# A hand-ordered RWKV-6 + SwiGLU kernel on one Trainium2 core: another order of the steps of its list

## The chip, the cores and the metric

The kernel runs on 1 core of one Trainium2 (trn2) chip. The metric is the device time of one execution in microseconds (us). Where the text names an engine by a short name, PE is TensorE (matmuls; PEld its weight loads), DVE is VectorE, ACT is ScalarE, POOL is GpSimd and SP is SyncE, which here only issues transfers.

## The reference

For every batch b (4), head h (8) and time t (768), with vectors r, k, v, w of 48 elements, an attention with a decaying state:

```python
for t in range(S):
    cur = np.einsum('bhd,bhe->bhde', u[None] * kt, vt)
    y[:, :, t] = np.einsum('bhd,bhde->bhe', rt, state + cur)
    state = wt[:, :, :, None] * state + np.einsum('bhd,bhe->bhde', kt, vt)
```

Then y, laid out as 3072 tokens of 384 features, goes through an RMS norm with gain and a SwiGLU network with 1536 hidden units:

```python
xn = x / np.sqrt(np.mean(x * x, -1, keepdims=True) + 1e-06) * rms_g
g = xn @ w_gate
out = (g * (1 / (1 + np.exp(-g))) * (xn @ w_val)) @ w_out
```

## The kernel before

Time is cut into 6 superblocks n = 0 to 5 of 128 steps; a superblock holds the 4 batches j = 0 to 3, so 512 tokens. In a superblock the attention goes batch by batch: the running sum of ln w becomes a matmul with a triangular mask (`ln`, `cs_mm`), its exponentials scale r and k (`exp_r`, `exp_k`, `r_mul`, `k_mul`), both are transposed (`rk_pe` and `rk_tr`), q k^T is formed and masked (`q_mm`, `q_mask_e`, `q_mask_o`), and `y_mm` adds the part of the block itself and the part of the carried state (`st_mm`, `st_new` make the next state). The u-term goes by POOL (`bonus_mul`, `bonus_v`) with a sum on DVE (`bonus_sum`). `x_add`, `x_sq`, `x_rstd`, `xn_mul`, `xn_pe`, `xn_out` make the normed and transposed tokens. When all four batches of a superblock have these, its network starts: 12 pairs of `gate_mm` and `val_mm` (three matmuls of 512 columns each), `silu` on ACT, `h_mul` on DVE, then `o_mm` (12 matmuls) for each batch, `o_out` and `out_dma`. The attention of superblock n+1 is woven into the network of superblock n.

Everything goes in the order of one list: `ORDER` (L25 to L126) has one word for each step, function.n.j, and L648 calls them one after the other. No scheduler moves anything. Each engine keeps the order of the steps that are its own, and waits, at its next step, for whatever that step's inputs and buffers need; nothing behind it on that engine passes. So the list sets five queues at once:

- SP issues the loads of r, k, v (L211) and w (L228), 192 KB each, the transposes by DMA of superblocks 2 to 5, and the stores.
- POOL issues the weights of the network (`load_gv`, L313: gate and value; `load_wo`, L319: w_out in three parts), between its own work: `bonus_mul` (L423, L424), `bonus_v` (L433), `q_mask_o` (L476), from superblock 2 on the casts of v. The `load_wo` also wait until load_v.1.1 has landed.
- PE's PSUM buffers come from three pools: `psA` (2, for gate and cs), `psB` (2, for val and cs) and `psQ` (4, for all the rest). A pool hands its buffers out in turn, in the order of the list: a step that takes a psQ buffer waits until the taker four before it has been read out.
- In superblocks 0 and 1 the casts of v (`cast_v`, L337) and the copies of the transposes out of PSUM (`rk_tr`, L449) are ACT's, and the norm's `x_rstd` of superblock 0 also (two small activations on L198). All exp, ln and silu are recorded on L198, their table loads on L196.
- DVE does `w_tot` (L409), `r_mul` (L412), `k_mul` (L417), `bonus_sum` (L428), `q_mask_e` (L465), `q_mask_o` of superblock 0 (L473), `st_new` (L492 and L494), `x_add` (L511), `xn_out` (L551), `h_mul` (L584) and half of `o_out` (L636).

The calls of `load_wo`, and the wait that goes with them:

```python
WO_BEHIND = (('load_v', 1, 1), ('load_v', 1, 1), ('load_v', 1, 1))
```

## Time and profile before

| | us |
|---|---|
| median of 6 runs | 207.83 |
| lowest and highest run | 206.96, 208.36 |
| the profiled execution: its own time | 208.21 |
| the profiled execution: its span, first to last instruction | 206.5 |

So 1.71 us of the profiled execution lie around its span, and that execution is 0.38 us above the median. Its mean granted TensorE clock is 0.958 of full speed.

The steps can be placed on the trace, since each engine keeps the order of the list. The marks that matter here, in us from the start of the span: the first network starts (gate_mm.0.0) at 28.60; the second part of its weights is used first (gate_mm.0.4) at 37.12; the last gate (gate_mm.0.11) at 49.97 to 50.78; its first `o_mm` starts at 53.77; the second network starts at 65.25, the third at 95.06, the fourth at 124.97, the fifth at 153.11, the sixth at 171.94; the last matmul ends at 203.3.

How to read it: the profile gives each engine's busy time, in 40 slices of the span too; the view by stages gives the same for stretches that the reader chooses; the chain of waits goes back from the last instruction to what released each one; the DMA view gives what each queue moved in a stretch (q1 carries what SP issues, q0 what POOL issues).

### The profile page before, as it was taken

The numbers are of one execution on the slowest core, as the hardware profiler recorded it, in microseconds if no ns is written. First come the engines' busy times: TensorE is split into PE (matmuls) and PEld (weight loads), VectorE is DVE, ScalarE is ACT, GpSimd is POOL, SyncE is SP. The second block draws the span as 40 slices with busy tenths as digits, with TensorE's granted clock in tenths as the row PEclk, the third lists the DMA queues.
The fourth block names the chain that finished last, engine by engine and source line by source line (L and its number), as shares of the span: only waits on it lengthen the run. The fifth ranks groups of instructions, "written<-read, shape, count | busy, mean of one in ns | idle before, by whom it ended". The sixth has DMA issues, their size and how long they took to land.

```text
span 206.5 us, 4369 instructions
## 1 busy us (share of the span) xinstructions
PE 191.2 (93%) x1524; PEld 111.2 (54%) x1524; DVE 158.6 (77%) x323; ACT 138.4 (67%) x282; POOL 108.1 (52%) x167
## 2 busy tenths in 40 slices
PE   4667889898999999999999999999999999999993
...
DVE  6498845778999899999999989899997955246411
...
PEclk9995558999999999999999999999999999999999
...
GB/s 133 218 212 202 185 201 203 175 166 227 186 204 223 177 211 229 207 235 201 170 212 251 122 185 211 202 233 106 38 153 203 42 38 3 76 0 40 0 119 76
DMA packets 125728, 32.41 MB, mean 157 GB/s; under 512 B 120581, under 2 KB 124553, under 8 KB 125705
## 3 DMA queue, kind: packets, MB, share of 16 engines
...
## 4 chain that ended last, share of the span: by engine, by line
PE 71%; SPq 19%; ACT 3%; DMA 3%; issue 1%; DVE 1%; ACTq 0%; DVEq 0%
PE ps_q L629 21%; PE ps_a L566 20%; PE ps_b L566 19%; SPq L211 16%; SPq L228 3%; DMA rt<-in_r_dram 3%; PE ps_q L458 2%; PE ps_q L503 2%; PE ps_q L506 2%; PE ps_a L378 1%; PE ps_q L486 1%; PE ps_q L540 1%; ACT lw L198 1%; ACT L196 1%; PE ps_a L381 1%
## 5 line engine op out<-in xcount | busy, mean ns | idle before, releaser
L584 DVE TENSOR_TENSOR ht<-ps_b,sg 128x512 bf16<-128x512 f32 x72 | 49.0, 688 | 20.6 <-PE ps_b L566 14.3
L198 ACT ACTIVATE sg<-ps_a 128x512 bf16<-128x512 f32 x72 | 42.9, 597 | 32.9 <-PE ps_a L566 30.3
L566 PE MATMUL ps_a<-xnt,wg_sb 128*128 128x512 bf16 x216 | 59.7, 386 | 1.0 <-DMA wg_sb<-in_moe_w_gate_dram 1.0
L566 PE MATMUL ps_b<-xnt,wv_sb 128*128 128x512 bf16 x216 | 59.2, 383 | 0.0
L629 PE MATMUL ps_q<-wo_sb,ht 128*128 128x384 bf16 (+1 forms) x300 | 50.1, 319 | 0.0
L629 PEld LDWEIGHTS <-ht 128*128 128x128 bf16 x300 | 28.0, 97 | 16.4
L423 POOL TENSOR_TENSOR ruk<-rt,kt 128x384 f32<-128x384 f32 x24 | 24.6, 1024 | 22.9 <-DMA rt<-in_r_dram 14.2
L566 PEld LDWEIGHTS <-wv_sb 128*128 128x128 bf16 x216 | 23.7, 114 | 20.9 <-issue 2.0
L566 PEld LDWEIGHTS <-wg_sb 128*128 128x128 bf16 x216 | 23.3, 115 | 21.3 <-issue 1.8
L424 POOL TENSOR_TENSOR ruk<-ruk,u_bc 128x384 f32<-128x384 f32 x24 | 23.9, 998 | 1.9
L476 POOL TENSOR_SCALAR_AFFINE_SELECT qts<-qts 128x512 bf16<-128x512 bf16 x20 | 12.7, 634 | 15.6 <-ACT qts L469 15.6
L433 POOL TENSOR_TENSOR ydiag<-vt,diag 128x384 f32<-128x384 f32 x24 | 19.8, 829 | 0.6 <-DVE diag L428 0.5
L465 DVE TENSOR_TENSOR qts<-ps_q,mask_lt 128x512 bf16<-128x512 f32 x24 | 16.4, 683 | 2.1 <-PE ps_q L460 1.7
L529 ACT ACTIVATE xn<-xb,rstd 128x384 bf16<-128x384 f32 x24 | 14.4, 608 | 2.1 <-POOL rstd L525 1.9
L198 ACT ACTIVATE lw<-wt 128x384 bf16<-128x384 f32 x24 | 12.1, 517 | 4.6 <-DMA wt<-in_w_dram 4.6
L469 ACT CAST qts<-ps_q 128x512 bf16<-128x512 f32 x20 | 11.6, 582 | 4.5 <-PE ps_q L460 4.5
L511 DVE TENSOR_TENSOR xb<-ps_q,ydiag 128x384 f32<-128x384 f32 x24 | 13.2, 551 | 1.8 <-PE ps_q L506 1.7
L196 ACT ACT_TABLE_LOAD x10 | 12.8, 1283 | 1.8 <-PEq L665 1.6
L636 DVE COPY ob<-ps_q 128x384 f32<-128x384 f32 (+1 forms) x13 | 7.0, 539 | 8.5 <-PE ps_q L629 8.5
L516 ACT ACTIVATE junk<-xb 128x384 bf16<-128x384 f32 x24 | 12.5, 519 | 1.5 <-DVE xb L511 1.2
L428 DVE TENSOR_REDUCE diag<-ruk 128x8 f32<-128x384 f32 x24 | 12.9, 544 | 0.0
L417 DVE TENSOR_TENSOR rk<-kt,ps_b 128x384 bf16<-128x384 f32 x20 | 11.0, 548 | 2.4 <-ACT ps_b L198 2.1
...
## 6 DMA issues: line engine op xcount, KB each, us to landing
...
```

What stands on the lines that cost most here:

```text
L196: nc.scalar.preload_act_table_set(table_name)
L198: return nc.scalar.activation(**kw).ins
L211: dmas["load_" + which, n, j] = nc.sync.dma_start(out=inp[which, n, j], in_=t[j, :, n * L:(n + 1) * L, :].rearrange("h t d -> t h d")).ins
L423: nc.gpsimd.tensor_tensor(out=ruk[n, j], in0=inp["r", n, j], in1=inp["k", n, j], op=ALU.mult)
L424: nc.gpsimd.tensor_tensor(out=ruk[n, j], in0=ruk[n, j], in1=u_bc, op=ALU.mult)
L433: nc.gpsimd.tensor_tensor(out=ydiag[n, j], in0=inp["v", n, j], in1=diag[n, j].to_broadcast([128, H, D]), op=ALU.mult)
L465: nc.vector.tensor_tensor(out=qts[n, j][:, 0], in0=bank["q", n, j][0], in1=bc_mid(mask_lt, NP), op=ALU.mult)
L511: nc.vector.tensor_tensor(out=xb[n, j], in0=bank.pop(("y", n, j)), in1=ydiag[n, j].rearrange("p h d -> p (h d)"), op=ALU.add)
L529: nc.scalar.activation(out=xn, in_=xb[n, j], func=AF.Copy, scale=rstd[n, j][:, 1:2])
L566: nc.tensor.matmul(ps, lhsT=units(ws, c, f), rhs=xnt[n][:, c, :], start=(c == 0), stop=(c == KC - 1))
L584: nc.vector.tensor_tensor(out=ht[n][:, f, :], in0=bank.pop(("v", n, f)), in1=bank.pop(("sg", n, f)), op=ALU.mult)
L629: nc.tensor.matmul(ps[:, cols], lhsT=ht[n][:, f, b * L:(b + 1) * L], rhs=wo_sb[:, f, cols], start=(f == 0), stop=(f == FC - 1))
```

## The change

The list `ORDER` is written anew; it has the same 1063 steps, and nothing else in the kernel changes. Line numbers behind the list move down by one. By engine:

- SP: the first 26 loads (through load_v.1.1) keep their order. Then load_r.1.2, load_k.1.2, load_r.1.3, load_k.1.3 come in this order, where before both k came first. load_v.1.2 goes ahead of load_w.2.1; load_k.2.0 and load_w.2.2 go ahead of load_v.1.3; load_r.2.0 goes from ahead of load_w.2.1 to behind load_v.1.3; the transpose rk_tr.2.0 goes from ahead of load_k.2.2 to behind load_k.2.3. Later, out_dma.3.2 and 3.3 go behind the four xn_tr of superblock 5.
- POOL: the order is the same through bonus_mul.1.0, all four `load_gv` included. Then bonus_v.1.0 comes ahead of bonus_mul.1.1; load_wo.0.0 comes right behind bonus_mul.1.1, and load_wo.2.0 and load_wo.1.0 come behind bonus_mul.1.2 (before: 2.0 and 1.0 ahead of bonus_mul.1.2, and 0.0 behind q_mask_o.1.0); bonus_mul.1.3 comes ahead of q_mask_o.1.0 and q_mask_o.1.1.
- ACT: exp_r.1.0 goes forward by 12 places, to behind cast_v.0.1; x_sq.0.0 goes behind both; ln.1.1 goes behind x_rstd.0.0; cast_v.0.2 goes behind rk_tr.0.3 and cast_v.0.3 behind exp_k.1.0 and x_sq.0.1; ln.1.3 goes ahead of x_rstd.0.2; exp_r.1.2 ahead of exp_k.1.2. In the first network rk_tr.1.0 comes ahead of silu.0.3. Later ln.2.3 goes behind xn_mul.1.3. The number of table loads stays 10.
- DVE: in superblock 0 q_mask_e.0.1, w_tot.0.2, q_mask_o.0.1 and bonus_sum.0.1 come ahead of x_add.0.0; st_new.0.1 and x_add.0.1 ahead of bonus_sum.0.2. In the first network the steps of superblock 1 follow the new order of the loads: before, k_mul.1.2, k_mul.1.3, r_mul.1.2, st_new.1.0, r_mul.1.3 follow each other, with h_mul steps between; now r_mul.1.2, k_mul.1.2, r_mul.1.3, st_new.1.0, k_mul.1.3.
- PE: st_mm.0.1 and y_mm.0.1 come ahead of rk_pe.0.3 and q_mm.0.2; st_mm.0.3 goes from ahead of cs_mm.1.2 to behind gate_mm.0.1; q_mm.1.0 goes ahead of gate_mm.0.4; rk_pe.1.1 goes behind val_mm.0.7, rk_pe.1.3 and st_mm.1.1 behind gate_mm.0.10; cs_mm.2.1 goes behind y_mm.1.3; q_mm.2.0 goes behind val_mm.1.1. In superblocks 2 to 4 y_mm.2.0, y_mm.3.0 and q_mm.3.2 come 7 to 11 places earlier and a few others move by 1 to 5; from gate_mm.4.0 on, o_mm.4.1 and o_mm.4.2 move by 1 and 3 places and the rest by one at most.
- At the end o_out.4.1 goes from behind silu.5.1 to behind silu.5.10, and o_out.4.2 from behind h_mul.5.6 to behind h_mul.5.11.

The part of the diff for superblocks 0 and 1:

```diff
@@ ORDER, superblocks 0 and 1 @@
-load_w.0.0 load_v.0.0 load_w.0.1 load_k.0.0 load_r.0.0 ln.0.0 load_w.0.2 load_r.0.1 ln.0.1 cs_mm.0.0 load_k.0.1
-cs_mm.0.1 exp_k.0.0 load_w.0.3 exp_r.0.0 k_mul.0.0 bonus_mul.0.0 exp_r.0.1 r_mul.0.0 exp_k.0.1 load_r.0.2 w_tot.0.0
-cast_v.0.0 rk_pe.0.0 ln.0.2 load_k.0.2 st_mm.0.0 r_mul.0.1 rk_tr.0.0 cs_mm.0.2 load_w.1.0 st_new.0.0 bonus_mul.0.1
-q_mm.0.0 k_mul.0.1 load_v.0.1 w_tot.0.1 bonus_sum.0.0 ln.0.3 rk_pe.0.1 exp_k.0.2 q_mask_e.0.0 load_k.0.3 exp_r.0.2
-cs_mm.0.3 q_mask_o.0.0 bonus_v.0.0 rk_tr.0.1 load_r.0.3 y_mm.0.0 k_mul.0.2 bonus_mul.0.2 exp_k.0.3 q_mm.0.1 load_w.1.1
-r_mul.0.2 exp_r.0.3 x_add.0.0 ln.1.0 rk_pe.0.2 load_v.0.2 bonus_sum.0.1 x_sq.0.0 q_mask_e.0.1 cast_v.0.1 bonus_v.0.1
-load_v.0.3 w_tot.0.2 rk_tr.0.2 q_mask_o.0.1 cs_mm.1.0 k_mul.0.3 load_w.1.2 q_mm.0.2 bonus_sum.0.2 bonus_mul.0.3
-r_mul.0.3 load_k.1.0 q_mask_o.0.2 ln.1.1 rk_pe.0.3 x_rstd.0.0 load_w.1.3 cast_v.0.2 y_mm.0.1 bonus_v.0.2 rk_tr.0.3
-load_r.1.0 x_add.0.1 load_gv.0.0 q_mask_e.0.2 cast_v.0.3 load_r.1.1 xn_mul.0.0 bonus_sum.0.3 load_gv.0.1 q_mm.0.3
-ln.1.2 y_mm.0.2 bonus_v.0.3 x_sq.0.1 q_mask_e.0.3 st_mm.0.1 exp_k.1.0 w_tot.0.3 x_add.0.2 load_gv.1.1 cs_mm.1.1
-x_rstd.0.1 q_mask_o.0.3 exp_r.1.0 load_gv.1.0 x_sq.0.2 y_mm.0.3 exp_k.1.1 xn_pe.0.0 x_add.0.3 st_mm.0.2 x_rstd.0.2
-st_new.0.1 xn_mul.0.1 x_sq.0.3 st_new.0.2 st_mm.0.3 load_v.1.0 cs_mm.1.2 x_rstd.0.3 xn_out.0.0 xn_mul.0.2 xn_pe.0.1
-xn_mul.0.3 xn_out.0.1 xn_pe.0.2 ln.1.3 xn_pe.0.3 xn_out.0.2 exp_r.1.1 xn_out.0.3 exp_k.1.2 cs_mm.1.3 k_mul.1.0
-exp_r.1.2 gate_mm.0.0 st_new.0.3 exp_k.1.3 exp_r.1.3 val_mm.0.0 silu.0.0 gate_mm.0.1 h_mul.0.0 val_mm.0.1 silu.0.1
-gate_mm.0.2 h_mul.0.1 val_mm.0.2 silu.0.2 gate_mm.0.3 val_mm.0.3 load_k.1.1 silu.0.3 load_v.1.1 r_mul.1.0
-bonus_mul.1.0 load_k.1.2 h_mul.0.2 rk_pe.1.0 gate_mm.0.4 h_mul.0.3 load_k.1.3 rk_tr.1.0 r_mul.1.1 val_mm.0.4
-load_r.1.2 silu.0.4 bonus_sum.1.0 gate_mm.0.5 bonus_mul.1.1 k_mul.1.1 q_mm.1.0 load_r.1.3 silu.0.5 val_mm.0.5
-h_mul.0.4 cast_v.1.0 load_w.2.0 q_mask_e.1.0 gate_mm.0.6 q_copy_o.1.0 load_wo.2.0 h_mul.0.5 rk_pe.1.1 load_r.2.0
-st_mm.1.0 k_mul.1.2 val_mm.0.6 load_wo.1.0 rk_tr.1.1 k_mul.1.3 gate_mm.0.7 bonus_mul.1.2 silu.0.6 r_mul.1.2 val_mm.0.7
-silu.0.7 h_mul.0.6 gate_mm.0.8 cast_v.1.1 load_w.2.1 st_new.1.0 rk_pe.1.2 bonus_v.1.0 val_mm.0.8 rk_tr.1.2 q_mm.1.1
-h_mul.0.7 q_mask_o.1.0 gate_mm.0.9 silu.0.8 r_mul.1.3 load_wo.0.0 q_copy_o.1.1 val_mm.0.9 bonus_sum.1.1 silu.0.9
-rk_pe.1.3 h_mul.0.8 bonus_v.1.1 st_mm.1.1 gate_mm.0.10 rk_tr.1.3 q_mask_e.1.1 bonus_mul.1.3 load_v.1.2 val_mm.0.10
-h_mul.0.9 silu.0.10 st_new.1.1 gate_mm.0.11 y_mm.1.0 silu.0.11 q_mm.1.2 q_mask_o.1.1 x_add.1.0 ln.2.0 val_mm.0.11
-q_mask_e.1.2 load_v.1.3 q_mm.1.3 h_mul.0.10 y_mm.1.1 load_k.2.0 h_mul.0.11 q_copy_o.1.2 cs_mm.2.0 bonus_sum.1.2
-x_sq.1.0 q_mask_o.1.2 o_mm.0.0 load_k.2.1 bonus_sum.1.3 q_copy_o.1.3 x_rstd.1.0 x_add.1.1 ln.2.1 load_w.2.2
-q_mask_e.1.3 exp_r.2.0 q_mask_o.1.3 cast_v.1.2 r_mul.2.0 load_w.2.3 cs_mm.2.1 x_sq.1.1 bonus_v.1.2 o_out.0.0 st_mm.1.2
-xn_mul.1.0 y_mm.1.2 st_new.1.2 x_rstd.1.1 load_r.2.1 o_mm.0.1 cast_v.1.3 bonus_mul.2.0 xn_mul.1.1 load_r.2.2 x_add.1.2
-exp_k.2.0 x_sq.1.2 k_mul.2.0 st_mm.1.3 y_mm.1.3 exp_r.2.1 st_new.1.3 rk_tr.2.0 o_mm.0.2 o_out.0.1 bonus_v.1.3
-exp_k.2.1 ln.2.2 x_rstd.1.2 x_add.1.3 ln.2.3 load_k.2.2 w_tot.2.0 k_mul.2.1 load_r.2.3 xn_pe.1.0 xn_mul.1.2 xn_pe.1.1
-o_out.0.2 cs_mm.2.2 x_sq.1.3 xn_out.1.0 xn_pe.1.2 load_k.2.3 o_mm.0.3 exp_r.2.2 w_tot.2.1 x_rstd.1.3 xn_out.1.1
-exp_k.2.2 load_v.2.0 r_mul.2.1 bonus_mul.2.1 xn_mul.1.3 r_mul.2.2 out_dma.0.0 xn_out.1.2 xn_pe.1.3 cs_mm.2.3 w_tot.2.2
-xn_out.1.3 q_mm.2.0 rk_tr.2.1 exp_k.2.3 k_mul.2.2 gate_mm.1.0 bonus_mul.2.2 exp_r.2.3 bonus_sum.2.0 val_mm.1.0
...
+load_w.0.0 load_v.0.0 load_w.0.1 load_k.0.0 load_r.0.0 ln.0.0 load_w.0.2 load_r.0.1 cs_mm.0.0 ln.0.1 load_k.0.1
+cs_mm.0.1 exp_k.0.0 exp_r.0.0 load_w.0.3 k_mul.0.0 exp_r.0.1 bonus_mul.0.0 r_mul.0.0 exp_k.0.1 w_tot.0.0 load_r.0.2
+cast_v.0.0 rk_pe.0.0 ln.0.2 st_mm.0.0 load_k.0.2 rk_tr.0.0 cs_mm.0.2 r_mul.0.1 st_new.0.0 load_w.1.0 q_mm.0.0
+bonus_mul.0.1 k_mul.0.1 load_v.0.1 w_tot.0.1 bonus_sum.0.0 rk_pe.0.1 ln.0.3 q_mask_e.0.0 exp_k.0.2 load_k.0.3
+cs_mm.0.3 exp_r.0.2 q_mask_o.0.0 bonus_v.0.0 rk_tr.0.1 load_r.0.3 y_mm.0.0 k_mul.0.2 bonus_mul.0.2 exp_k.0.3 q_mm.0.1
+r_mul.0.2 exp_r.0.3 load_w.1.1 ln.1.0 rk_pe.0.2 q_mask_e.0.1 load_v.0.2 w_tot.0.2 q_mask_o.0.1 cast_v.0.1 cs_mm.1.0
+bonus_sum.0.1 load_v.0.3 x_add.0.0 exp_r.1.0 bonus_v.0.1 load_w.1.2 st_mm.0.1 x_sq.0.0 y_mm.0.1 r_mul.0.3
+bonus_mul.0.3 rk_tr.0.2 k_mul.0.3 load_k.1.0 st_new.0.1 x_rstd.0.0 rk_pe.0.3 load_w.1.3 ln.1.1 x_add.0.1 q_mm.0.2
+xn_mul.0.0 bonus_sum.0.2 rk_tr.0.3 load_r.1.0 w_tot.0.3 q_mask_e.0.2 bonus_v.0.2 q_mask_o.0.2 cast_v.0.2 load_r.1.1
+q_mm.0.3 load_gv.0.0 exp_k.1.0 bonus_sum.0.3 cs_mm.1.1 x_sq.0.1 load_gv.0.1 q_mask_e.0.3 cast_v.0.3 xn_pe.0.0
+q_mask_o.0.3 x_rstd.0.1 bonus_v.0.3 y_mm.0.2 load_v.1.0 xn_out.0.0 xn_mul.0.1 st_mm.0.2 load_gv.1.1 y_mm.0.3 x_add.0.2
+ln.1.2 exp_k.1.1 x_add.0.3 cs_mm.1.2 load_gv.1.0 x_sq.0.2 k_mul.1.0 x_sq.0.3 xn_pe.0.1 ln.1.3 xn_out.0.1 x_rstd.0.2
+st_new.0.2 x_rstd.0.3 xn_mul.0.2 xn_mul.0.3 xn_pe.0.2 exp_r.1.1 xn_pe.0.3 xn_out.0.2 exp_r.1.2 cs_mm.1.3 xn_out.0.3
+exp_k.1.2 exp_r.1.3 gate_mm.0.0 exp_k.1.3 val_mm.0.0 silu.0.0 gate_mm.0.1 load_k.1.1 h_mul.0.0 st_mm.0.3 val_mm.0.1
+silu.0.1 bonus_mul.1.0 st_new.0.3 gate_mm.0.2 r_mul.1.0 val_mm.0.2 silu.0.2 h_mul.0.1 rk_pe.1.0 h_mul.0.2 gate_mm.0.3
+rk_tr.1.0 bonus_sum.1.0 val_mm.0.3 silu.0.3 q_mm.1.0 q_copy_o.1.0 load_v.1.1 load_r.1.2 gate_mm.0.4 r_mul.1.1
+val_mm.0.4 load_k.1.2 q_mask_e.1.0 cast_v.1.0 bonus_v.1.0 gate_mm.0.5 h_mul.0.3 silu.0.4 load_r.1.3 bonus_mul.1.1
+k_mul.1.1 silu.0.5 val_mm.0.5 load_k.1.3 h_mul.0.4 gate_mm.0.6 cast_v.1.1 h_mul.0.5 load_w.2.0 val_mm.0.6 silu.0.6
+r_mul.1.2 load_wo.0.0 gate_mm.0.7 load_v.1.2 h_mul.0.6 st_mm.1.0 bonus_mul.1.2 val_mm.0.7 silu.0.7 k_mul.1.2 rk_pe.1.1
+r_mul.1.3 gate_mm.0.8 h_mul.0.7 val_mm.0.8 load_wo.2.0 silu.0.8 st_new.1.0 load_w.2.1 rk_pe.1.2 rk_tr.1.1 load_wo.1.0
+gate_mm.0.9 rk_tr.1.2 q_mm.1.1 k_mul.1.3 bonus_mul.1.3 val_mm.0.9 bonus_sum.1.1 silu.0.9 gate_mm.0.10 h_mul.0.8
+rk_pe.1.3 h_mul.0.9 silu.0.10 q_mask_o.1.0 st_mm.1.1 val_mm.0.10 q_mask_e.1.1 q_copy_o.1.1 load_k.2.0 rk_tr.1.3
+st_new.1.1 gate_mm.0.11 q_mask_o.1.1 y_mm.1.0 bonus_v.1.1 silu.0.11 q_mm.1.2 x_add.1.0 ln.2.0 val_mm.0.11 q_mask_e.1.2
+q_mm.1.3 h_mul.0.10 y_mm.1.1 load_w.2.2 h_mul.0.11 q_copy_o.1.2 cs_mm.2.0 load_v.1.3 q_mask_e.1.3 x_sq.1.0 o_mm.0.0
+q_copy_o.1.3 x_add.1.1 x_rstd.1.0 load_r.2.0 exp_r.2.0 bonus_sum.1.2 cast_v.1.2 q_mask_o.1.2 bonus_sum.1.3 ln.2.1
+load_w.2.3 bonus_v.1.2 x_sq.1.1 st_mm.1.2 y_mm.1.2 o_out.0.0 load_k.2.1 o_mm.0.1 q_mask_o.1.3 st_new.1.2 ln.2.2
+x_rstd.1.1 exp_k.2.0 load_k.2.2 cast_v.1.3 x_add.1.2 bonus_v.1.3 load_r.2.1 k_mul.2.0 st_mm.1.3 x_sq.1.2 y_mm.1.3
+st_new.1.3 xn_mul.1.0 cs_mm.2.1 x_rstd.1.2 load_r.2.2 o_mm.0.2 o_out.0.1 exp_r.2.1 bonus_mul.2.0 w_tot.2.0 load_r.2.3
+r_mul.2.0 exp_k.2.1 x_add.1.3 xn_mul.1.1 out_dma.0.0 k_mul.2.1 xn_mul.1.2 cs_mm.2.2 o_out.0.2 x_sq.1.3 xn_pe.1.0
+xn_pe.1.1 load_k.2.3 w_tot.2.1 xn_pe.1.2 xn_out.1.0 exp_r.2.2 o_mm.0.3 x_rstd.1.3 exp_k.2.2 xn_out.1.1 rk_tr.2.0
+r_mul.2.1 bonus_mul.2.1 xn_mul.1.3 xn_out.1.2 ln.2.3 w_tot.2.2 r_mul.2.2 xn_pe.1.3 load_v.2.0 cs_mm.2.3 xn_out.1.3
+rk_tr.2.1 exp_r.2.3 k_mul.2.2 bonus_mul.2.2 gate_mm.1.0 exp_k.2.3 r_mul.2.3 val_mm.1.0 w_tot.2.3 silu.1.0 k_mul.2.3
...
```

## The prediction

> **What bounds the kernel now.** First the page: who is busy, and where along the span.
>
> ```profile
> PE 191.2 (93%) x1524; PEld 111.2 (54%) x1524; DVE 158.6 (77%) x323; ACT 138.4 (67%) x282; POOL 108.1 (52%) x167
> ...
> PE   4667889898999999999999999999999999999993
> ...
> DVE  6498845778999899999999989899997955246411
> ...
> PEclk9995558999999999999999999999999999999999
> ```
>
> PE is full from the tenth slice on and lacks work only in the first 50 us, where its clock is also halved for three slices. DVE is nearly as full from there to slice 28. Order alone can win time only where both stand still, so the view by stages comes next (columns: stretch, length, busy us of PE, PEld, DVE, ACT, POOL, granted clock).
>
> ```profile
> 28.60:32.10 3.50, 3.50 (x10) 1.27 (x9) 1.14 (x4) 2.75 (x4) 1.40 (x2) 0.50 1.12 202
> 32.20:37.10 4.90, 3.92 (x24) 2.11 (x22) 2.63 (x5) 2.73 (x4) 0.49 (x1) 1.00 1.14 211
> 37.10:47.40 10.30, 10.23 (x72) 5.29 (x72) 7.53 (x14) 7.11 (x13) 7.07 (x8) 1.00 0.90 168
> 47.40:53.80 6.40, 5.73 (x72) 3.63 (x72) 6.29 (x13) 4.47 (x7) 3.98 (x7) 1.00 1.14 226
> 53.80:84.30 30.50, 30.42 (x266) 17.86 (x265) 28.92 (x62) 22.54 (x48) 24.45 (x37) 1.00 1.05 205
> 84.30:114.80 30.50, 29.97 (x262) 17.70 (x259) 29.89 (x65) 22.69 (x47) 24.08 (x35) 1.00 1.03 214
> ```
>
> PE's idle time is 0.98 us ahead of 37.1 and 0.67 between 47.4 and 53.8; behind that 0.08 and 0.53 in 30.5 us each, and 0.39 in the next 32.0. The time to be had lies between 28 and 54. The chain of waits says what ended it there:
>
> ```profile
> 38.85 2.43 SPq L211
> ...
> 41.32 6.08 DMA rt<-in_r_dram
> ...
> 47.43 0.57 DVE rk L412
> ...
> 48.04 0.62 PE ps_q L440 x8
> ...
> 51.43 1.28 ACT L196
> ...
> 53.88 2.00 PE ps_q L629 x12
> ```
>
> load_r.1.3 takes 6.08 us to land, r_mul.1.3 waits for it, rk_pe.1.3 for that; then the network's last pairs, a table load, ln.2.0, o_mm.0.0. The DMA view of 44 to 46 us says why it takes so long:
>
> ```profile
> q0 software_dynamic: 118, 0.34, 90.5%
> q1 hardware_dynamic: 188, 0.03, 10.8%
> ```
>
> load_wo.2.0 and 1.0 (POOL's queue q0, issued at 41.76 and 42.36) move eleven times what SP's queue moves.
>
> **The change part by part.** "Before" is the profiled execution (208.21 us, span 206.5).
>
> *0 to 14 us.* Every engine keeps its order: nothing.
>
> *14 to 28.6 us (ACT's order).* Before, ACT stands 0.96 us ahead of ln.1.1 (17.41) and 0.25 ahead of ln.1.2 (20.92), both for loads of w. Now ln.1.1 stands behind rk_tr.0.2 and x_rstd.0.0, and ln.1.2 later: these waits go. A new one comes. On DVE, from 14.03 (end of r_mul.0.2), go q_mask_e.0.1, w_tot.0.2, q_mask_o.0.1, bonus_sum.0.1 and x_add.0.0, at the steps from start to start of before (0.60, 0.07, 0.60, 0.46, then 0.55): 16.3. So x_sq.0.0 starts at 16.35 (before 14.53), though exp_r.1.0 already uses 0.4 of that time, and rk_tr.0.2 ends at 17.9 (before 16.45). From there to the start of exp_r.1.1 ACT has what it had from 17.41 to 27.32, 9.91 us, less the wait of 0.25 and less exp_r.1.0 (0.37): 17.9 + 9.3 = 27.2, for 27.32. The casts of v.0.2 and v.0.3 end at about 20.9 and 22.4 instead of 18.8 and 20.15; y_mm.0.2 and 0.3 wait for their masks (20.9 and 22.7 by the same counting) anyhow. gate_mm.0.0 so moves by -0.1. Ends: -1.2 (both waits gone, nothing new) and +0.9 (x_sq.0.0's 1.8 us less the 0.96).
>
> *28.6 to 37.1 us.* gate_mm.0.4 waits for the second part of the weights, 0.99 us on PE, and that landing doesn't follow PE: where PE starts 0.1 earlier nothing is won. bonus_sum.0.2 now ends at about 19.4 (behind st_new.0.1 and x_add.0.1; before 17.14), bonus_v.0.2, which ended at 19.51 ahead of load_gv.0.0, ends at 20.2: load_gv.0.0 is issued up to 0.75 later; the last two load_gv (22.03, 22.83) wait for bonus_v.0.3, whose sum ends 0.7 later, so they move by 0.2. The landing is at 37.1 to 37.9. In the wait PE now does st_mm.0.3 (0.31) and q_mm.1.0 (0.33), the second of which stood behind gate_mm.0.4.
>
> *37 to 50 us, by the loads.* The four loads landed one after the other: their users started at 42.07, 42.83, 43.59 and 47.43. Of the 3.84 us before the last, q0 is the cause: in 43.0 to 47.41 it moved 0.56 MB. Now only load_wo.0.0 is issued at about 41.8, a third of w_out's 1.18 MB (0.56 + 0.62 by the two stretches to 53 us), 0.39; the other two come behind bonus_mul.1.2, that is 42.83 + 2.3 = 45.1 to 46.3, and took 2 us to start flowing. So 0.17 MB less stands ahead, at 0.17 MB/us (0.34 in 2 us): the fourth load (now k.1.3) lands 1.0 earlier, at 46.4. DVE reaches it in time: r_mul.1.2 42.07, h_mul.0.6, k_mul.1.2, r_mul.1.3, h_mul.0.7 (0.69, 0.56, 0.56, 0.69 with overlap), st_new.1.0 (1.3) to 46.05; then k_mul.1.3, bonus_sum.1.1, h_mul.0.8 to 48.05, which was 49.05.
>
> *37 to 50 us, by PE.* From gate_mm.0.4 to the end of gate_mm.0.11 stand, at the steps from start to start that such groups show at the full clock, 15 gate or val groups of 0.648 (9.72), three rk_pe of 0.454, q_mm.1.1 of 0.33, two st_mm of 0.17: 11.75 us. Before it was 0.33 more, and took 50.78 - 37.12 = 13.66. New wait: q_mm.1.1's second psQ buffer is now the one that st_new.1.0 frees (46.05; before a step long done): 0.45 behind gate_mm.0.9's 45.65. From 37.12 that gives 49.3; from 37.9 the wait is covered and it gives 49.65; by DVE's h_mul.0.8 (which frees the buffer of val_mm.0.10) 48.1 + 1.35 = 49.45. I take 49.6, a gain of **1.1** (ends 0 and -1.6, its 13.66 less 11.75 and 0.3).
>
> *50 to 54 us.* silu.0.11, table load, ln.2.0, q_copy_o.1.2 follow gate_mm.0.11 as before, so o_mm.0.0 starts 1.1 earlier, 52.7. Cover: y_mm.1.0 needs q_mask_o.1.0, now behind bonus_mul.1.3 (46.4 + 2.0 + 0.64 = 49.05; needed 49.5). The last part of w_out, issued at 46.3, took 5.5 to 7.4 to land: 51.8 to 53.7; o_mm.0.0 needs its second third at 52.7 + 0.65 = 53.35. If that cover is gone, 0.4.
>
> *Behind 54 us.* q_mm.2.0 (0.33) passes behind two pairs, xn_mul.1.3 loses 0.45 of ACT work ahead of it (ln.2.3), which must come in time for cs_mm.2.3: at most PE's small gaps there, 0.8. Superblocks 2 to 4 are reordered between full engines: PE's idle time there, 0.08 + 0.53 + 0.39, is all that can go, and DVE (29.89 of 30.5 busy) has 0.6 us of slack in that stage before a stall costs. At the end o_out.4.1 and 4.2 (192 to 194.5) still free their psQ buffers before o_mm.5.1 (197.23) and 5.2 (199.18), and out_dma.3.2 and 3.3 have no reader: nothing. I take 0 for all this, ends -0.8 and +0.9 (gaps of the other sign, by the same rows).
>
> Sum: -1.1. Of the profiled execution 208.21 it leaves 207.1; that one stands 0.38 above the median, so 206.7 us.
>
> [...] In the nine us from 26 to 35, q0 moved 1.63 MB in 925 packets and q1 0.17 MB in 920. [...] The clock is 0.50 until 32.1 and 1.00 from 32.2, 3.5 us behind the first dense group. [...]
>
> **The rivals.**
> 1. *The wait only changes its place* (20%): k.1.3 lands at 47.4 all the same since one part of w_out starves SP's queue too, or the weights at 37.9 and q_mm.1.1's new wait add up. Against: a third less ahead of it. 0: 207.8, from 207.3 to 208.4.
> 2. *The hole behind* (19%, slower): load_wo.2.0 and 1.0 now flow together at about 48 to 52.3, ahead of load_w.2.1, k.2.0, w.2.2, v.1.3. SP's queue then moves 0.19 MB/us (1.33 MB in 53 to 60), 1.03 us a load, so they land at 53, 54, 55, 56. ACT comes to ln.2.2 at 55.2 and cast_v.1.3 at 56.2, with nothing to spare. Each us later than that stops ACT, and x_sq, xn_mul and the second network behind it. With the landings 2 to 3 us later than that (a load stuck in a hole took 6.08) ACT loses 2 to 3, less 1.1: +0.9 to +1.9, with losses behind 54 us up to +2.3. It decides from load_w.2.2 landing at 55.2. 209.1.
> 3. *More than the forecast* (11%): load_gv.0.0 later lets r.1.0 and r.1.1 (issued at 19.9 and 20.8, used at 30.6 and 37.4) land ahead of the weights, ACT's new order saves its 1.2, and PE's gaps ahead of the second network (0.8) go: -2.0, 205.8.
>
> **The numbers.** The forecast has 50%: 206.7, by its own bounds 205.9 to 207.2. About 0.5% (1.04 us) is what a measurement of this kernel can tell from no change; faster is below 206.79, slower above 208.87. Of the forecast's 50%, 31 lie below 206.79 and 19 above; rival 3 adds 11 to faster, rival 1 gives 16 to same and 4 to slower, rival 2 gives 19 to slower: faster 0.42, same 0.35, slower 0.23. The range for 8 in 10 reaches from rival 3 to rival 2: 205.6 to 209.0.
>
> **What would show it.** The marks: gate_mm.0.0 at 28.5, gate_mm.0.4 at 37.1 to 37.9, k_mul.1.3 starting at 46.4, gate_mm.0.11 ending at 49.6, o_mm.0.0 at 52.7, the second network at 64.1, all later marks 1.1 earlier than before. ACT should show no wait of 0.9 for w.1.1. Wrong: k_mul.1.3 at 47.4 or later (rival 1), ACT idle ahead of ln.2.2 or cast_v.1.3 with a DMA as releaser (rival 2), or marks that drift back behind 65 us through PE waiting on DVE.

## The result, and the profile after

| | kernel before | changed kernel |
|---|---|---|
| median, us | 207.67 (50 runs) | 208.92 (24 runs) |
| lowest and highest run, us | 206.45, 209.93 | 207.97, 211.75 |
| ratio | | 1.0067, 95% interval 1.0048 to 1.0085 |

The change made the kernel 0.67% slower, 1.4 us; forecast was 1.1 us faster. A median here is over all runs, while a ratio leaves out runs over 1.5% above the fastest of their kernel: three of the changed kernel's 24, and in experiment 2 five of the twelve of e2_gv_before and three of the six of e2_gv_after, which took 211.6 to 218.2 us. The changed kernel's first profiled execution took 211.51 us, with one more half-clock stretch of TensorE than most; so the profile read here is a second one of the same kernel, of 209.47 us (span 207.8). Line numbers of the changed kernel are one higher than before.

Its page, the lines that answer to those of before:

```profile
PE 190.5 (92%) x1524; PEld 112.2 (54%) x1524; DVE 162.0 (78%) x323; ACT 138.1 (66%) x282; POOL 108.3 (52%) x167
...
PE   4694779798999999999999899999999999999993
...
DVE  6499828699999899999899999978997865325411
...
PEclk9999999999999999999999999999999999999999
```

DVE is busy 3.4 us longer (162.0 for 158.6) with the same 323 instructions: some of them take longer than before. The nines of PEclk do not mean a full clock from the start. The timeline of PE has the first matmuls of the network (start, duration):

```profile
28.87 1.44 PE L567 MATMUL ps_a<-xnt,wg_sb 128*128 128x512 bf16 x3
30.10 1.40 PE L567 MATMUL ps_b<-xnt,wv_sb 128*128 128x512 bf16 x3
31.34 0.81 PE L567 MATMUL ps_a<-xnt,wg_sb 128*128 128x512 bf16 x3
```

gate_mm.0.0 takes 1.44 us here as it did in the kernel before (28.60 to 30.04, at a clock of 0.50), and the same three matmuls take 0.81 us from 31.34 on. So TensorE ran at half speed up to about 31.3 us in this execution too, and the row does not show it; from there on the clock was full. The view by stages, cut at this kernel's own marks (columns as before: PE, PEld, DVE, ACT, POOL, clock):

```profile
32.20:37.90 5.70, 4.31 (x34) 2.12 (x31) 3.92 (x7) 3.29 (x5) 1.77 (x2) 1.00 1.15 212
37.90:47.40 9.50, 8.86 (x54) 4.78 (x54) 9.11 (x13) 5.25 (x9) 7.51 (x9) 1.00 0.94 179
47.40:54.90 7.50, 6.67 (x81) 4.23 (x82) 7.34 (x14) 5.81 (x10) 3.66 (x5) 1.00 1.09 213
54.90:85.50 30.60, 30.35 (x267) 18.07 (x266) 29.17 (x62) 22.80 (x49) 25.88 (x38) 1.00 1.09 211
```

Between 37.9 and 54.9 DVE is now the full engine (16.45 of 17.0 us), and PE idles 1.47 us. The chain of waits of the stretch from 26 to 60 us begins with a load of r, load_r.1.1: r_mul.1.1 waits 2.01 us for it and starts at 38.25, where it started at 37.41 before. Behind that no load of r or k is in it, but these three are, each a multiplication of 0.56 us in the kernel before:

```profile
21.30 16.93 DMA rt<-in_r_dram
38.25 0.56 DVE rk L413
...
39.93 1.01 DVE rk L418
...
44.69 1.34 DVE rk L413
...
47.89 1.25 DVE rk L418
```

The timeline of DVE (start, duration, line) shows k_mul.1.1, k_mul.1.2, r_mul.1.3 and k_mul.1.3:

```profile
39.93 1.37 DVE L418 TENSOR_TENSOR rk<-kt,ek 128x384 bf16<-128x384 f32 x1
...
43.49 1.26 DVE L418 TENSOR_TENSOR rk<-kt,ek 128x384 bf16<-128x384 f32 x1
44.68 1.35 DVE L413 TENSOR_TENSOR rk<-rt,er 128x384 bf16<-128x384 f32 x1
...
47.89 1.31 DVE L418 TENSOR_TENSOR rk<-kt,ek 128x384 bf16<-128x384 f32 x1
```

and that of POOL the two multiplications of bonus_mul.1.1, 1.2 and 1.3:

```profile
39.89 1.00 POOL L424 TENSOR_TENSOR ruk<-rt,kt 128x384 f32<-128x384 f32 x1
...
43.34 1.00 POOL L424 TENSOR_TENSOR ruk<-rt,kt 128x384 f32<-128x384 f32 x1 [0.62 <-DMA kt<-in_k_dram]
44.42 1.20 POOL L425 TENSOR_TENSOR ruk<-ruk,u_bc 128x384 f32<-128x384 f32 x1
...
47.79 1.00 POOL L425 TENSOR_TENSOR ruk<-ruk,u_bc 128x384 f32<-128x384 f32 x1
```

Each long one starts while POOL multiplies, and ends 0.41 us after that POOL instruction: 40.89 and 41.30, 44.34 and 44.75, 45.62 and 46.03, 48.79 and 49.20. Adding r_mul.1.0 (1.35 us, beside bonus_mul.1.0), five instructions cost 3.8 us more than 0.56 each. In the kernel before the order was the other way round: DVE began 0.11 us ahead, and it was POOL that took longer, 1.31 and 1.30 us where its other multiplications take 1.00:

```profile
38.91 0.56 DVE L417 TENSOR_TENSOR rk<-kt,ek 128x384 bf16<-128x384 f32 x1 [0.48 <-DMA kt<-in_k_dram]
...
43.59 0.56 DVE L412 TENSOR_TENSOR rk<-rt,er 128x384 bf16<-128x384 f32 x1 [0.20 <-DMA rt<-in_r_dram]
```
```profile
39.02 1.31 POOL L423 TENSOR_TENSOR ruk<-rt,kt 128x384 f32<-128x384 f32 x1 [6.33 <-DMA kt<-in_k_dram]
...
43.70 1.30 POOL L423 TENSOR_TENSOR ruk<-rt,kt 128x384 f32<-128x384 f32 x1 [0.80 <-DMA rt<-in_r_dram]
```

Why only in superblock 1? The view by source line of the changed kernel (min/median/max ns) splits k_mul by its operands: in superblock 1 the exponential (`ek`, `er`) lies in SBUF, in the others in PSUM (`ps_b`), and those 20 take 544 to 555 ns. They had POOL beside them too: in the first profile of the change one starts at 64.36, inside a multiplication of POOL (64.18 to 65.19), and takes 0.54 us.

```profile
L418 DVE TENSOR_TENSOR rk<-kt,ps_b x20: 544/545/555, 6.6 to 155.0; 128x384 bf16<-128x384 f32 x20
...
L418 DVE TENSOR_TENSOR rk<-kt,ek x4: 548/1287/1373, 24.0 to 47.9; 128x384 bf16<-128x384 f32 x4
```

In these rows the instruction that begins second is the long one, VectorE's in the changed kernel (1.26 to 1.37 us for 0.56), GpSimd's in the kernel before (1.31 and 1.30 us for 1.00), and both have all their inputs in SBUF (for an exception see the last section).

Two theories went into the experiments. **Port**, which is only a name, since no run shows what the two engines share: the held multiplications are the loss. **Weights**: the other visible difference, the second part of the weights at 37.91 instead of 37.12 (POOL issued load_gv.0.0 at 20.03 instead of 19.45), is the loss. The port theory came only after experiment 1; the expectations there set a loads theory against the weights, which puts the loss between gate_mm.0.4 and gate_mm.0.11, by the new order of the loads and q_mm.1.1's wait.

### The profile page after: what moved, and what is told of

Its sections match the earlier page's. It is cut to its first block, busy times and chain, and to the rows that moved or that the text cites. A ratio compares the mean times of both kernels' runs of the same rounds, so it can differ in the third digit from the quotient of the medians.

```text
span 209.8 us, 4378 instructions
## 1 busy us (share of the span) xinstructions
PE 189.7 (90%) x1524; PEld 110.7 (53%) x1524; DVE 160.7 (77%) x323; ACT 138.1 (66%) x282; POOL 108.1 (52%) x167
## 4 chain that ended last, share of the span: by engine, by line
PE 65%; DMA 10%; DVE 6%; SPq 6%; ACT 6%; issue 3%; POOL 2%; DVEq 0%; ACTq 0%; POOLq 0%
PE ps_a L567 21%; PE ps_b L567 20%; PE ps_q L630 18%; DMA wg_sb<-in_moe_w_gate_dram 7%; SPq L212 4%; SPq L229 3%; DMA vt<-in_v_dram 2%; PE ps_q L459 2%; ACT L197 2%; DVE rk L413 1%; PE ps_q L507 1%; PE ps_q L504 1%; ACT sg L199 1%; DVE ht L585 1%; PE ps_a L379 1%
## 5 line engine op out<-in xcount | busy, mean ns | idle before, releaser
L199 ACT ACTIVATE sg<-ps_a 128x512 bf16<-128x512 f32 x72 | 42.4, 595 | 36.4 <-PE ps_a L567 35.9
L567 PE MATMUL ps_a<-xnt,wg_sb 128*128 128x512 bf16 x216 | 60.5, 390 | 2.3 <-DMA wg_sb<-in_moe_w_gate_dram 2.1
L567 PE MATMUL ps_b<-xnt,wv_sb 128*128 128x512 bf16 x216 | 59.9, 387 | 0.0
L567 PEld LDWEIGHTS <-wg_sb 128*128 128x128 bf16 x216 | 23.8, 115 | 23.7 <-issue 3.2
L567 PEld LDWEIGHTS <-wv_sb 128*128 128x128 bf16 x216 | 23.0, 115 | 20.2 <-issue 1.4
L425 POOL TENSOR_TENSOR ruk<-ruk,u_bc 128x384 f32<-128x384 f32 x24 | 24.4, 1016 | 1.9
L517 ACT ACTIVATE junk<-xb 128x384 bf16<-128x384 f32 x24 | 12.5, 521 | 5.6 <-DVE xb L512 5.4
L199 ACT ACTIVATE lw<-wt 128x384 bf16<-128x384 f32 x24 | 12.2, 516 | 4.1 <-DMA wt<-in_w_dram 4.1
L525 POOL TENSOR_SCALAR rstd<-rstd 128x1 f32<-128x1 f32 x20 | 3.8, 190 | 18.4 <-ACT junk L517 18.1
```

The costliest lines, as they stand in the source:

```text
L199: return nc.scalar.activation(**kw).ins
L425: nc.gpsimd.tensor_tensor(out=ruk[n, j], in0=ruk[n, j], in1=u_bc, op=ALU.mult)
L567: nc.tensor.matmul(ps, lhsT=units(ws, c, f), rhs=xnt[n][:, c, :], start=(c == 0), stop=(c == KC - 1))
```

## The experiments

Times below are medians, and ratios those to the kernel before run beside them. The runs of one kernel spread over 1.4 us (e1_again) to 8.6 us (e2_gv_before; the 250.82 us of e1_middle aside), so the marks in the traces and the times are both given.

### 1. The change in three parts

Each kernel takes one stretch of the list from the change and the rest from before.

```diff
-ORDER = before
+ORDER = change up to gate_mm.0.0, then before        (e1_front)
+ORDER = before up to gate_mm.0.0, change up to gate_mm.1.0, then before   (e1_middle)
+ORDER = before up to gate_mm.1.0, then change        (e1_tail)
```

The changed kernel again:

> The changed kernel once more, for an undisturbed profile beside the three parts that run with it. Its ratio to the kernel before should be 1.005 to 1.009 again. Weights theory (POOL issues load_gv.0.0 about 1.2 us later, since bonus_v.0.2 waits for bonus_sum.0.2 on DVE, and the second part of the gate weights lands later): gate_mm.0.4 starts at 38.5 to 39 instead of 37.12, and TensorE stands about 2 us ahead of it. Loads theory (the new order of r.1.x, k.1.x, w_out and the psQ wait of q_mm.1.1): gate_mm.0.4 starts by 37.9 and the loss comes between it and gate_mm.0.11.

The front:

> Order of the change up to gate_mm.0.0, order of before from there on. Weights theory: this part alone carries the loss, ratio 1.004 to 1.009, gate_mm.0.4 at 38.5 to 39. Loads theory: ratio 0.998 to 1.001, gate_mm.0.4 by 37.9. The forecast's own terms for this part: gate_mm.0.0 at 28.5, total -0.1.

The middle:

> Order of before up to gate_mm.0.0, order of the change from there to gate_mm.1.0, then before again. Weights theory: the middle itself is worth something, ratio 0.994 to 1.000 (the forecast's -1.1 us would be 0.995), gate_mm.0.4 at 37.1, k_mul.1.3 at 46.4. Loads theory: ratio 1.004 to 1.009, with gate_mm.0.4 at 37.1 and k_mul.1.3 at 48 or later.

The tail:

> Order of before up to gate_mm.1.0, order of the change behind it. Both theories, and the forecast's step for this part: 0, ratio 0.998 to 1.002. If neither theory holds and the loss is the reordering of superblocks 2 to 5, ratio 1.004 or more.

| | median | ratio, 95% interval | gate_mm.0.4 starts | r_mul, k_mul of superblock 1 over 0.56 in sum |
|---|---|---|---|---|
| change | 209.22 | 1.0033 (1.0007 to 1.0059) | 37.91 | 3.8 |
| front | 210.45 | 1.0077 (1.0031 to 1.0123) | 38.45 | 0 |
| middle | 209.60 | 1.0046 (1.0014 to 1.0078) | not used | 3.0 |
| tail | 209.18 | 1.0031 (0.9998 to 1.0064) | 37.20 | 0 |

The shares add up to 1.5%, the whole to 0.3 to 0.7%: the parts are not independent, and no single part is the culprit by this test. The front came out as the weights theory had it (1.004 to 1.009, gate_mm.0.4 at 38.5 to 39), with no long multiplication in its profile; the middle's ratio came out as the loads theory had it (1.004 to 1.009); the change itself stayed below the 1.005 to 1.009 expected of it. The front's runs spread from 208.28 to 211.65. The middle's profiled execution was an odd one (250.82 us, clock 0.75); only who ran beside whom is taken from it. What does stand: the long multiplications come with the middle of the change, not with its front or tail.

### 2. The overlap taken away, and the weights issued earlier

Four waits keep bonus_mul behind the DVE instructions that it ran beside (e2_apart); load_gv.0.0 and 0.1 go ahead of bonus_v.0.2 in the changed kernel (e2_gv_after), in both together (e2_both), and in the kernel before (e2_gv_before).

```diff
+    MUL_BEHIND = {(1, 0): ('r_mul', 1, 0), (1, 1): ('k_mul', 1, 1), (1, 2): ('r_mul', 1, 3), (1, 3): ('k_mul', 1, 3)}
...
-        nc.gpsimd.tensor_tensor(out=ruk[n, j], in0=inp["r", n, j], in1=inp["k", n, j], op=ALU.mult)
+        i = nc.gpsimd.tensor_tensor(out=ruk[n, j], in0=inp["r", n, j], in1=inp["k", n, j], op=ALU.mult).ins
+        if (n, j) in MUL_BEHIND:
+            behind(i, dmas[MUL_BEHIND[n, j]])
```
```diff
-bonus_v.0.2 ... load_gv.0.0 ... load_gv.0.1
+load_gv.0.0 load_gv.0.1 bonus_v.0.2
```

> The changed kernel, with four waits that keep GpSimd's bonus_mul of superblock 1 behind the r_mul or k_mul of VectorE that it ran beside (1.0 behind r_mul.1.0, 1.1 behind k_mul.1.1, 1.2 behind r_mul.1.3, 1.3 behind k_mul.1.3). Port theory: the five VectorE multiplications that took 1.26 to 1.37 us in the changed kernel take 0.56 again, gate_mm.0.11 ends at 49.4 to 49.9 (37.9 + 11.75), 2 us earlier than in the changed kernel, o_mm.0.0 starts at 52.7 to 53.2; time about 2 us below the changed kernel, ratio to the kernel before 0.993 to 0.998. Weights theory: gate_mm.0.4 at 37.9 to 39 sets what follows, the multiplications being short does not help; ratio 1.002 to 1.006 as in the changed kernel.

> The changed kernel with load_gv.0.0 and 0.1 issued ahead of bonus_v.0.2, so at 18.6 us instead of 20.0. Weights theory: the second part of the weights lands 0.6 to 1.4 us earlier, gate_mm.0.4 at 36.5 to 37.4, and the time falls by as much: ratio 0.998 to 1.001. Port theory: gate_mm.0.4 comes earlier, but VectorE's 3 us of held multiplications between 39 and 49 stay and set gate_mm.0.11, which ends at 51.2 to 51.9; ratio 1.001 to 1.006.

> Both edits together: the four waits, and load_gv.0.0 and 0.1 ahead of bonus_v.0.2. Port theory: TensorE's 11.75 us from gate_mm.0.4 at 36.5 to 37.4 follow, gate_mm.0.11 ends at 48.3 to 49.3; ratio 0.988 to 0.995, below the kernel before. Weights theory alone: as the changed kernel with the early load_gv, 0.998 to 1.001.

> The kernel before with load_gv.0.0 and 0.1 ahead of bonus_v.0.2, issued at 18.7 us instead of 19.45. Says what an issue 0.75 us earlier is worth by itself. If the landing follows the issue: gate_mm.0.4 0.5 to 0.75 us earlier, ratio 0.996 to 0.998. If the transfers are limited by what SyncE's queue moves beside them, or r.1.3's landing sets the end of the stage anyway: 0.999 to 1.001.

With the waits: 207.87 us, ratio 0.9998 (0.9973 to 1.0024); the sum over 0.56 falls from 3.8 to 0.3 us. Its expected ratio, 0.993 to 0.998, was missed: in this run the loss went, but the gain did not come. The three kernels with the earlier issue: 212.35 us, 1.0151 (1.0088 to 1.0213); 211.74 us, 1.0147 (1.0090 to 1.0204); 208.42 us, 1.0002 (0.9966 to 1.0038). Neither theory had expected the first two; the third, in the kernel before, came out as level as one of its two expectations said. The waits of ACT between 20 and 36 us, in e2_both, say why:

```profile
ACT lw L199 <- DMA wt<-in_w_dram: 6.2, 1, 6.2
```

For its load of w ln stands 6.2 us (2.4 in e2_gv_after), while the DMA moves 203 and 201 GB/s (24 to 28 and 28 to 32 us), and the first network starts 6.0 us (2.3) later. That the weights, issued at 18.5 us, go ahead of this load, which SP issues at the same time, is the author's reading; these views do not show the order of the two. So issuing the weights earlier is no cure. It is no test of the weights theory either: the second part of the weights did land earlier (36.18 in e2_gv_after, 36.29 in e2_both, 37.86 in the change), but TensorE came to it only later, at 39.23 and 42.04.

The third kernel shows one thing more. Its DVE and POOL have the order of before, only with the two loads ahead, but r_mul.1.0 and bonus_mul.1.0 waited for their load of r until 36.5, and then r_mul.1.1 started inside a multiplication of POOL (38.21, in 38.03 to 39.03) and took 1.23 us instead of 0.56. So which engine is held depends on when a load lands, too, and not on the list alone.

### 3. The waits again, and without the change's front or tail

```diff
+ORDER = before up to gate_mm.0.0, change with the waits up to gate_mm.1.0, then before   (e3_mid_apart)
+ORDER = change with the waits up to gate_mm.1.0, then before                             (e3_front_mid)
```

> The changed kernel with the four waits again, for an undisturbed profile. Port theory: r_mul and k_mul of superblock 1 at 0.55 to 0.75 us; gate_mm.0.11 ends at about gate_mm.0.4 + 11.75 us; ratio 0.997 to 1.001 as in the first run of this kernel, so 0.3 to 0.7% below the changed kernel. Where the loss that is left sits is to be read from gate_mm.0.0 and gate_mm.0.4: if the front of the change is its place, gate_mm.0.4 starts at 37.9 or later.

> Order of before up to gate_mm.0.0, order of the change with the four waits from there to gate_mm.1.0, then order of before. Beside the middle part without the waits (1.0046). Port theory, with the forecast's sum for this stage: gate_mm.0.4 at 37.1, no multiplication over 0.8 us, gate_mm.0.11 ends at 49.0 to 49.6, ratio 0.992 to 0.996. If the order of the loads or the psQ wait of q_mm.1.1 costs as much as the port: 0.998 to 1.004.

> Order of the change with the four waits up to gate_mm.1.0, then order of before: the kernel of the four waits without the change's superblocks 2 to 5. Port theory and the forecast (0 behind 54 us): the same as the kernel with the four waits, 0.997 to 1.001. If the order behind 65 us costs, as the tail alone (1.0031, its interval reaching to 0.9998) leaves open: 0.994 to 0.997.

e3_apart: 207.67 us, 1.0030 (1.0001 to 1.0059). The other two, 208.63 us, 1.0069 (1.0035 to 1.0103), and 209.17 us, 1.0108 (1.0068 to 1.0148), were faulty as tests: the change puts the transpose rk_tr.2.0 later, and the old tail has q_mm.2.0 ahead of gate_mm.1.0, so that PE waits 1.9 and 0.9 us for it. The middle of experiment 1 has the same order there, though its one profile, at a clock of 0.75, shows no such wait. One thing they did show: in the first, gate_mm.0.11 started at 48.27, 1.70 us ahead of the first profile of before, and its silu at 49.11, 0.34 us ahead of the second (experiment 5).

### 4. Old front, with and without the waits

Behind gate_mm.0.0 these keep the change's own order. The third tries another way to the weights: bonus_sum.0.2 back ahead of st_new.0.1, so that load_gv.0.0 is issued as before.

```diff
+ORDER = before up to gate_mm.0.0, then change                    (e4_oldfront)
+ORDER = before up to gate_mm.0.0, then change with the waits     (e4_old_apart)
+... bonus_sum.0.2 st_new.0.1 ... (change with the waits)         (e4_sum_early)
```

> Order of before up to gate_mm.0.0, then the change's own order to the end (no waits added). If the front of the change carries its loss (weights at 37.9 and the half-speed stretch): gate_mm.0.4 at 37.1, no half-speed stretch behind 35 us, ratio 0.998 to 1.001. If the held multiplications carry it: r_mul and k_mul of superblock 1 still 2 to 4 us over their 0.56 in sum, gate_mm.0.11 ends at 51 to 52, ratio 1.003 to 1.007.

> Order of before up to gate_mm.0.0, then the change's order with the four waits to the end. Both causes taken away: gate_mm.0.4 at 36.8 to 37.2, gate_mm.0.11 ends at 48.9 to 49.3 (the trace of the middle with the waits had it start at 48.27), gate_mm.1.0 at 63.6 to 64.0, ratio 0.990 to 0.995, the best of all. If the forecast's gain for the stage is lost again behind 54 us (hole behind: SyncE's loads of superblock 2 late): gate_mm.1.0 at 64.5 or later, ratio 0.997 to 1.001.

> The changed kernel with the four waits, and bonus_sum.0.2 of VectorE ahead of st_new.0.1 and x_add.0.1, as in the kernel before: load_gv.0.0 is issued at about 19.4 again instead of 20.2. If the late issue is what makes the front cost: gate_mm.0.4 at 37.0 to 37.5, time 0.5 to 1 us below the kernel with the four waits alone, ratio 0.992 to 0.997. If not (the transfers of the stage are limited by what all queues move together): gate_mm.0.4 at 37.9 or later, ratio 0.998 to 1.003.

The pair differs in the waits alone: 208.75 us, 1.0049 (1.0026 to 1.0072) without, 207.53 us, 1.0010 (0.9982 to 1.0039) with them. The first came out as expected of held multiplications (1.003 to 1.007). In the second gate_mm.0.11 ended at 49.51 and gate_mm.1.0 started at 63.86, near the marks expected (48.9 to 49.3, 63.6 to 64.0), but the time was not: 0.990 to 0.995 was missed. The timeline of the second, DVE and POOL:

```profile
42.42 0.54 DVE L418 TENSOR_TENSOR rk<-kt,ek 128x384 bf16<-128x384 f32 x1
42.89 0.55 DVE L413 TENSOR_TENSOR rk<-rt,er 128x384 bf16<-128x384 f32 x1
```
```profile
43.52 0.99 POOL L426 TENSOR_TENSOR ruk<-rt,kt 128x384 f32<-128x384 f32 x1 [1.49 <-DVE rk L413]
```

The two multiplications of DVE, 0.99 and 1.35 us without the waits, are short, and now it is POOL that waits; in the view of waits from 37 to 50 us no engine waits for POOL in turn. Of 2.4 us over 0.56 in the eight r_mul and k_mul, 0.5 are left. The two profiles differ in more than the hold: in the first r_mul.1.0 waited for its load until 35.09 (33.46 in the second), so that TensorE reached gate_mm.0.4 at 37.89 and 37.47, in both behind the landing of the weights (36.36 and 36.77); and the waits put load_wo.2.0 to 45.54 instead of 44.69. The third kernel took 208.03 us, 1.0022 (0.9996 to 1.0049), with load_gv.0.0 at 20.75 all the same: no verdict on the late issue.

### 5. The overlap put in on purpose, and the kernel before once more

Into e4_old_apart, behind load_wo.0.0: two multiplications of POOL that read SBUF, or five memsets that only write. Both go into a spare tile that nothing reads.

```diff
+        nc.gpsimd.tensor_tensor(out=spare, in0=ruk[1, 1], in1=u_bc, op=ALU.mult)    (e5_read, twice)
+        nc.gpsimd.memset(spare, 0.0)                                                (e5_write, five times)
```

> The kernel with the old front and the four waits, and behind load_wo.0.0 on GpSimd two further multiplications of 128x384 into a spare tile, with both inputs in SBUF (about 1 us each, 42.0 to 44.0). Port theory: k_mul.1.2 or r_mul.1.3, whichever start beside them, take 0.9 to 1.5 us instead of 0.55, and gate_mm.0.11 comes 0.4 to 1.0 us later than without (from 48.7 to 49.1 to 49.7). If the long multiplications had another cause (loads, semaphores): both stay at 0.55 and only bonus_mul.1.2 moves, by at most 0.5 us.

> The same kernel with five memsets of the spare tile in place of the two multiplications (about 0.4 us each, 2 us in sum), which write SBUF and read nothing. Port theory, in the form that it is the reading of SBUF that collides: k_mul.1.2 and r_mul.1.3 stay at 0.55, gate_mm.0.11 as without them. If any GpSimd work on SBUF holds VectorE: as with the multiplications.

> The kernel before, one more look. If its stage from gate_mm.0.4 to gate_mm.0.11 is set by the landing of load_r.1.3, that stage differs between executions: 12.84 us in the first one, 11.6 to 13.7 expected from kernels that share its order. If it is set by the engines: 12.8 again.

e5_read, DVE and POOL:

```profile
42.07 1.07 DVE L418 TENSOR_TENSOR rk<-kt,ek 128x384 bf16<-128x384 f32 x1
43.06 1.35 DVE L413 TENSOR_TENSOR rk<-rt,er 128x384 bf16<-128x384 f32 x1
```
```profile
41.70 2.30 POOL L434 TENSOR_TENSOR spare<-ruk,u_bc 128x384 f32<-128x384 f32 x2
```

The multiplications are long again, so in the trace the hold can be put in as well as taken away; from silu.0.4 to silu.0.11 this profile takes 12.03 us, for 11.04 without the two multiplications and 11.30 with the memsets. In e5_write no multiplication of DVE was held (two of POOL's, begun 0.05 and 0.10 us behind one of DVE, took 1.36 and 1.31 us): r_mul.1.3 took 0.55 beside a memset, but it had started 0.2 us ahead of it. That memset was not held either (all five took 418 to 442 ns), where a multiplication of POOL that began 0.11 us behind DVE took 1.30 us instead of 1.00. The other order, DVE second to an instruction that only writes, stays open. The times do not tell the pair apart: 208.85 us, 1.0055 (1.0027 to 1.0084), and 208.77 us, 1.0055 (1.0023 to 1.0087). The second has no held multiplication of DVE to explain it by, so the times of this pair say nothing for the port theory. The profiles show what the pair was limited by. The added work keeps POOL busy about 2.3 us longer, so it issues the last part of w_out later (46.14 without it), and the chain of waits of both kernels goes through its landing (e5_read, then e5_write):

```profile
47.10 7.00 DMA wo_sb<-in_moe_w_out_dram
```
```profile
49.15 6.85 DMA wo_sb<-in_moe_w_out_dram
```

In both o_mm waits 0.3 us for w_out, and in e5_write y_mm waits 1.7 us more for a mask of POOL (q_mask_o). From silu.0.11 to silu.1.0 they take 16.63 and 18.07 us, for 16.17 without the added work. The weights were not late in e5_write (they landed at 36.79): r_mul.1.0 waited for its load of r until 35.41, and TensorE reached gate_mm.0.4 at 38.20.

The kernel before, one more execution: 207.25 us. r_mul.1.3, which waited for its load until 47.43 in the first one, starts at 46.06, and the view shows no wait:

```profile
46.06 0.56 DVE L412 TENSOR_TENSOR rk<-rt,er 128x384 bf16<-128x384 f32 x1
```

### 6. With the old tail

Old front, middle of the change with the waits, order of before behind gate_mm.1.0.

```diff
+ORDER = (e4_old_apart) up to gate_mm.1.0, then before, with q_mm.2.0 behind val_mm.1.1
```

> Old front, middle of the change with the four waits, order of before behind gate_mm.1.0 with q_mm.2.0 behind val_mm.1.1. If the order behind 65 us costs 0.3 us: from silu.1.0 to silu.5.11 125.7 us instead of 126.0, ratio 0.994 to 0.999 (the kernel with the change's own tail had 1.0010). If not: 0.999 to 1.004.

207.68 us, 1.0022 (0.9995 to 1.0049). From silu.1.0 to silu.5.11 it took 126.5 us, not 125.7: what the old tail should have brought is not there. No version beat the kernel before; the best are level with it.

### The stages side by side

From the starts of silu, in us (silu.0.4 follows the second part of the weights, silu.0.11 the last gate of the first network):

| execution of | silu.0.4 at | 0.4 to 0.11 | 0.11 to 1.0 | 1.0 to 5.11 |
|---|---|---|---|---|
| before, first profile | 37.99 | 12.82 | 16.39 | 125.7 |
| before, second profile | 37.75 | 11.69 | 16.78 | 125.7 |
| before up to 65 us (e1_tail) | 38.08 | 13.62 | 16.39 | 126.3 |
| change (e1_again) | 39.41 | 12.52 | 16.21 | 126.0 |
| old front (e4_oldfront) | 38.92 | 12.15 | 16.21 | 126.3 |
| old front, waits (e4_old_apart) | 38.51 | 11.04 | 16.17 | 126.3 |
| waits, early sum (e4_sum_early) | 38.52 | 11.20 | 16.89 | 126.2 |
| old front, waits, old tail (e6_old_tail) | 38.04 | 10.84 | 16.59 | 126.5 |

With the waits the second column is 10.8 to 11.2, without them 12.2 to 12.5; before it is 11.7 to 13.6, by the landing of load_r.1.3 (e1_front and e2_gv_before, which have the order of before here, have 11.65 and 11.39). So by this column the change without the waits is no longer than before. The column starts late in the change: ACT waits 1.57 us for a load of v at cast_v.1.0, which now stands ahead of silu.0.4. From the start of gate_mm.0.4 to that of silu.0.11 it is 14.02 us in the change and 13.18 in e4_oldfront, 12.07 in each of the three kernels with the waits, and 12.5 to 14.5 in the five profiles with the order of before. (The two profiles of the change with the waits and its own front, 12.1 and 12.2, had a half-clock stretch in this column; see the last section.)

## Why the prediction was wrong, point by point

**The step that failed** is "37 to 50 us, by the loads", at "DVE reaches it in time: r_mul.1.2 42.07, h_mul.0.6, k_mul.1.2, r_mul.1.3, h_mul.0.7 (0.69, 0.56, 0.56, 0.69 with overlap), st_new.1.0 (1.3) to 46.05; then k_mul.1.3, bonus_sum.1.1, h_mul.0.8 to 48.05". The 0.56 came from one execution, in which each of them began ahead of POOL's multiplication or had none beside it. Measured: k_mul.1.2 1.26, r_mul.1.3 1.35, k_mul.1.3 1.31; st_new.1.0 ended at 47.86 and h_mul.0.8 at 50.39. gate_mm.0.11 ended at 51.90 instead of 49.6.

DVE also began late, at 38.25 behind load_r.1.1, but that alone does not make the end late: in e5_write r_mul.1.1 started later still, at 38.63, no multiplication of DVE was held, and h_mul.0.8 ended at 47.87 and silu.0.11 started at 50.53, for 50.39 and 51.93 in the change.

How much of the time the hold is, is less sure than that it is there. The one pair run side by side, the old front without and with the waits, has means 0.80 us apart (95% interval from resampling the runs, 0.24 to 1.33). With the change's own front, not run side by side, the ratios are 1.0033 and 1.0067 without the waits and 0.9998 and 1.0030 with them: 0.1 to 1.4 us. So about 0.8 of the 1.4 us, as an estimate from the one pair; the waits move a transfer of w_out by 0.85 us too, and the pair of experiment 5 could not decide it.

**The gain was counted from one execution.** The term that was mis-sized besides is the stage's "13.66" us. In that profile load_r.1.3 was late; in the second profile of before the stage takes 12.6 us (gate_mm.0.4 at 36.88, silu.0.11 at 49.45). With most of the hold gone the change's stage takes 12.0 us (37.47 to 49.51 in e4_old_apart), as forecast; but of the 1.1 us that this should bring, 0.5 are left against the second profile, or 0.65 by the table's column (11.69 and 11.04). So the kernels with the waits are level with before in time (0.9998, 1.0010) or a little slower (1.0030). The column behind silu.1.0 is 0.3 to 0.8 us longer in all of them, and the old tail did not bring it back; e1_front, with the order of before there, has 126.0 too. That part is not settled.

The other steps:

- *14 to 28.6 us*: half right. x_sq.0.0 at 16.11 (16.35 forecast), gate_mm.0.0 at 28.87 (28.5). ACT's wait for a load of w did not go: 0.6 us here, 1.0 in the first profile.
- *28.6 to 37.1 us*: right. load_gv.0.0 0.58 us later (up to 0.75), weights at 37.91 (37.1 to 37.9).
- *The loads*: right, or better: load_k.1.3 landed at 44.72 (46.4 forecast). In e4_old_apart k_mul.1.3 starts at 45.30, behind st_new.1.0 and not behind its load (46.4 forecast).
- *By PE*: the new wait of q_mm.1.1 on st_new.1.0 came, 0.7 us in the view of waits for 0.45 forecast, as st_new.1.0 was late itself.
- *50 to 54 us*: right in kind; o_mm.0.0 follows gate_mm.0.11 by 3.80 us in both kernels.
- *Behind 54 us*: 0 forecast, +0.1 in the trace (148.49 us from o_mm.0.0 to the last o_mm, 148.35 before, 148.11 in the second profile of before).
- *Rival 2, the hole behind*: not seen. ln.2.2 starts at 57.46 without a wait for a load. Only when the stage is really shorter does it show: e4_sum_early waits 0.4 us for a load of w and 0.6 us for w_out.
- *Rival 1*: its sign was there, k_mul.1.3 at 47.89 (47.4 or later), but not for its reason: the load had landed at 44.72, and DVE came late. Weights at 37.9 and q_mm.1.1's wait were there too; the forecast had both in its sum and still had 49.65.

**Still open**: the front's share, and with it the weights theory. With the waits the old front and the new one are level (207.53; 207.87 and 207.67), without them too (208.75; 209.22 and 208.92), but the front alone, with no hold, was the slowest of the three parts, 1.0077. In e4_oldfront the weights did land early, at 36.36, and the loss stayed (1.0049), so late weights are not the whole of it. That issuing load_gv late leaves the DMA idle is only read from the trace, not tested: in 15 to 20 us 0.94 MB moved instead of 1.06.
